# Attention in front of two MoE layers: 1/rms by a GpSimd power, and k^T v of two heads in the two halves of TensorE's columns

## The chip, the cores and the metric

One core of a Trainium2 chip runs the whole program. The time is in microseconds (us) of device time, from the start of the program to its end; lower is better. Before the change it is 1328.89 us (median of three runs, 1328.19 to 1331.12).

## What is computed

Three layers follow one another. The attention has no softmax; for 8 batches and 8 heads of 576 rows and 64 columns it is

```python
kv  = np.einsum('bhsd,bhse->bhde', k, v)          # 64 x 64 for each head
out = np.einsum('bhsd,bhde->bhse', q, kv)
rms = np.sqrt(np.mean(out * out, axis=-1, keepdims=True) + 1e-06)
x   = out / rms * g_norm                          # over the 64 columns of a head
```

Its result, 4608 tokens of 512 columns, goes through a first layer (h = x @ w_in, g = h * cos(h), g @ w_out, inner width 2048) and a second one (width 1024, with a softmax gate and a layer norm). Everything is float32.

## The kernel before

The program is one long list of tasks. Each task names its engine, an estimated duration, the buffers that it reads and writes, and a due time `at`. A planner (`Flow.run`) plays the list on model engines: of the tasks that can start first on an engine it takes the one with the earliest due time, and it emits the instructions in that order. On the chip every engine then runs its own list strictly in that order, and waits at an instruction whose data are not there yet. So an estimate in the planner sets an order and nothing else.

The two layers run over blocks of 512 tokens: 36 steps for each quarter of the first layer's inner width, four such passes, then 18 pairs of token tiles for the second layer. The attention is cut into slots, which the planner spreads over the first pass (`run_slots`, SLOTS per step), so that the attention of later tokens runs beside the first layer of earlier ones. Two kinds of slot matter here.

`kv_slots` (line 346) makes k^T v of a batch. The 8 heads are 4 pairs; the 64 columns of a pair's two heads stand side by side in 128 columns. One product of 128x128 therefore gives both heads' 64x64 blocks on its diagonal and two blocks that nobody needs. The 576 rows of a pair are five products (L358 four times, L360 once). All four pairs of a batch share one PSUM bank, and two ScalarE copies (L368) take the diagonal blocks out into `kvf`, whose other blocks are zero.

`tile_slots` (line 393) makes two tiles of 128 tokens. Each tile has a bank: q times kvf (L416), a square on ScalarE (L421), a sum over each head on VectorE (L422). Then, for both tiles at once, 1/rms on VectorE: two instructions that make a first guess (L429, L430) and three Newton rounds of three (L434, L437, L440), eleven in all on 128x16 elements. Then for each tile VectorE scales the products into `xn` (L458), TensorE transposes them back into the same bank (L463), and ScalarE takes the result out with the factor g (L469). The bank is free after that.

Banks are given out in turn by `next_bank` (line 341): the first six come from the four accumulators and the two banks named o and s, all later ones alternate between o and s. In the trace o and s are called ps_o, the accumulators ps_acc, the first layer's h ps_h; most buffers of the attention are called att, the spare ones xt.

For each block, `prep_x` splits x into a high and a low part (L564 on ScalarE, L569 on VectorE for the first three blocks and on GpSimd after that). `weights` turns the stored weights into float32 (L502 to L514) and splits them (L525, L527). A power on GpSimd is already used in the second layer, on 128x1 elements (L756).

Of the kernel before, what the change touches and what calls it, by code (L numbers as in the profile page):

```python
# [10 lines left out]
I32 = mybir.dt.int32  # L11
# [29 lines left out]
INV_2PI = float(1.0 / (2.0 * math.pi))  # L41
MAGIC = float(0x5F3759DF)

TINY = 0.17

# [17 lines left out]
class Flow:  # L63
# [92 lines left out]
def tile_kernel(ctx, tc, qkv, tail, g2, w1, w2, gl, out):  # L156
# [31 lines left out]
    for key in ("g2", "halfpi"):  # L188
        declare("const", key, 0, [P, 1])
    declare("const", "mhalf", 0, [P, 1])  # L190
    declare("const", "gl", 0, [P, NC])
# [27 lines left out]
    declare("att", "xn", 2, [P, DM])  # L219
    for n in ("ss", "y", "yt"):  # L220
        declare("att", n, 2, [P, 2 * H])

# [118 lines left out]
    def next_bank():  # L341
        n_bank[0] += 1
        early = ACC + ["o", "s"]
        return early[n_bank[0] - 1] if n_bank[0] <= len(early) else ("o", "s")[n_bank[0] % 2]

    def kv_slots(b):

        bk, n = next_bank(), ("kvf", b % 2)
        pairs = [("kvp", b, p) for p in range(NPAIR)]

        def slot(p):
# [10 lines left out]
            def copy(e):  # L362
                r = slice(e * D, (e + 1) * D)

                def blocks(key_):
                    return buf[key_][r, :].rearrange("p (n w) -> p n w", w=P)[:, :, r]

                ACT.copy(out=blocks(n), in_=blocks(bk))  # L368

            def run(at):  # L370
                kv_load(j, at - (ATT_LEAD if b else 0))
                if b == 0:
                    q_load(j, at)
                add("PE", 1.12, mm, r=[kv, tl] + ([bk] if p else []), w=[pairs[p]] + ([] if p else [bk]), at=at)
                if p == NPAIR - 1:
                    for e in range(2):
                        add("ACT", 0.4, lambda e=e: copy(e), r=[bk, *pairs], w=[("kvfh", n, e)] + ([n] if e == 0 else []), at=at)

            return run

        return [slot(p) for p in range(NPAIR)]

# [10 lines left out]
    def tile_slots(g):  # L393


        i = g % 2
        bks = [next_bank() for _ in range(2)]
        ss, y, yt = ("ss", i), ("y", i), ("yt", i)
        halves = [("ssh", g, h) for h in range(2)]

# [3 lines left out]
        def first(h, at):  # L404
            t, bk, sq = 2 * g + h, bks[h], stage()
            for b, a, n, row in parts(t):
# [6 lines left out]
                def mm(b=b, a=a, n=n, row=row, qs=qs, kvf=kvf):  # L413
                    for p in range(NPAIR):
# [3 lines left out]

                add("PE", 0.89, mm, r=[kvf, ("kvfh", kvf, 0), ("kvfh", kvf, 1), *qs], w=[bk], at=at)
            at -= PRI  # L420
            add("ACT", 0.61, lambda: ACT.activation(out=buf[sq], in_=buf[bk], func=AF.Square), r=[bk], w=[sq], at=at)  # L421
            add("DVE", 0.66, lambda: DVE.tensor_reduce(out=buf[ss][:, h * H:(h + 1) * H], in_=heads(buf[sq]), axis=AX.X,  # L422
                                                       op=ALU.add), r=[sq] + ([ss] if h else []),
                w=[halves[h]] + ([] if h else [ss]), at=at)


        def newton(at):
            def start():
                DVE.tensor_scalar(out=buf[ss], in0=buf[ss], scalar1=1.0 / D, scalar2=1e-6, op0=ALU.mult, op1=ALU.add)  # L429
                DVE.tensor_scalar(out=buf[y].bitcast(I32), in0=buf[ss].bitcast(I32), scalar1=-0.5, scalar2=MAGIC,  # L430
                                  op0=ALU.mult, op1=ALU.add)

            def square():
                DVE.tensor_tensor(out=buf[yt], in0=buf[y], in1=buf[y], op=ALU.mult)  # L434

            def times():
                DVE.scalar_tensor_tensor(out=buf[yt], in0=buf[yt], scalar=-0.5, in1=buf[ss], op0=ALU.mult, op1=ALU.mult)  # L437

            def update():
                DVE.scalar_tensor_tensor(out=buf[y], in0=buf[yt], scalar=1.5, in1=buf[y], op0=ALU.add, op1=ALU.mult)  # L440

            def all_():
                start()
                for _ in range(3):
                    square()
                    times()
                    update()

            add("DVE", 11 * TINY, all_, r=[*halves, ss], w=[ss, y, yt], at=at)

        def second_(h, at):
            t, bk, xn = 2 * g + h, bks[h], ("xn", h)

# [3 lines left out]
            def norm():  # L457
                DVE.tensor_tensor(out=heads(buf[xn]), in0=heads(buf[bk]),  # L458
                                  in1=buf[y][:, h * H:(h + 1) * H].unsqueeze(2).to_broadcast([P, H, D]), op=ALU.mult)

# [5 lines left out]
            xk = [x for k in range(KC) for x in xkeys(k, t * P, P)]  # L466
            add("DVE", 0.71, norm, r=[bk, y], w=[xn], at=at, ps=True)
# [4 lines left out]
        def run0(at):  # L472
            first(0, at)

        def run1(at):
            first(1, at)
            newton(at - PRI)
            for h in range(2):
                second_(h, at - PRI)

        return [run0, run1]

# [401 lines left out]
    for i in range(NPASS * NSTEP):  # L884
# [115 lines left out]
```

## Time and profile before

| | us |
|---|---|
| median of three runs | 1328.89 |
| the profiled execution | 1329.38 |
| its span, first to last instruction | 1327.6 |
| TensorE busy | 1295.1 (98%) |
| VectorE busy | 927.8 (70%) |
| ScalarE busy | 676.7 (51%) |
| GpSimd busy | 385.6 (29%) |

A busy time is the time in which at least one instruction of the engine was under way; matmuls overlap in their pipeline, so the durations of single ones add up to more than that. A float32 product with float32 operands is two instructions in the trace (two pieces, each with its own weight load, PEld), so the 160 products of k^T v are 320 instructions. The granted clock (PEclk) is a share of 2.4 GHz: 1.00 is that, 0.50 is 1.2 GHz. The bracket at the end of a row is idle time of the engine just before it, and what ended it.

### The profile page before, as it was taken

What the parts mean: (1) busy time and instruction counts of PE and PEld (TensorE: products, weight loads), DVE (VectorE), ACT (ScalarE), POOL (GpSimd) and SP (SyncE); (2) the same over time, 40 slices, a digit from 0 to 9 for tenths busy, and PEclk for the clock granted to TensorE, in tenths of its full rate; (3) what the DMA queues carried; (4) which work ended last, traced back from release to release, by engine and by line L of the source; (5) the groups of instructions that cost most, each with busy time, mean ns of one, the idle gap of its engine ahead of it and who ended that gap; (6) DMA issues with size and microseconds to landing.
All of it is one profiled execution on the core that took longest, in us unless ns stands there. A gap on an engine that the chain in (4) does not pass through costs nothing.

```text
span 1327.6 us, 17232 instructions
## 1 busy us (share of the span) xinstructions
PE 1295.1 (98%) x6148; PEld 1077.8 (81%) x6148; DVE 927.8 (70%) x1620; ACT 676.7 (51%) x1195; POOL 385.6 (29%) x364
## 2 busy tenths in 40 slices
PE   6789899999999999999999999999999999999998
PEld 6678788888888888888888888888788888888886
DVE  5889556588986456754545677878987878787853
ACT  3556445467655445545444555555554544444432
POOL 0001212036663225523131456443232212121100
PEclk9899999999999999999999999999999999999999
DMA  8643244323544243423232535464110111010000
GB/s 299 206 140 115 84 147 131 101 96 96 171 146 135 72 119 113 149 68 123 79 112 87 151 109 159 142 213 137 67 46 35 56 56 46 35 56 25 16 32 32
DMA packets 61830, 139.54 MB, mean 105 GB/s; under 512 B 7344, under 2 KB 9392, under 8 KB 60592
## 3 DMA queue, kind: packets, MB, share of 16 engines
q1 hardware_dynamic: 61744, 138.44, 32.4%
q8 instruction: 48, 0.79, 0.2%
q14 instruction: 38, 0.31, 0.1%
HBM read 91.23 MB, written 47.19 MB: 104 GB/s over the span
## 4 chain that ended last, share of the span: by engine, by line
PE 86%; DVE 6%; DMA 3%; ACT 2%; issue 1%; SPq 0%; POOL 0%; ACTq 0%; DVEq 0%
PE ps_acc L176 13%; PE ps_acc L174 13%; PE ps_acc L175 13%; PE ps_h L174 13%; PE ps_h L176 12%; PE ps_h L175 12%; PE ps_acc L773 2%; PE ps_o L416 2%; PE ps_o L358 2%; DMA xt<-w 2%; PE ps_o L463 1%; DVE att L440 1%; DVE att L437 1%; DVE att L434 1%; DMA xt<-qkv 1%
## 5 line engine op out<-in xcount | busy, mean ns | idle before, releaser
L569 POOL TENSOR_TENSOR xhl<-xt,xhl 128x512 fp32r<-128x512 f32 (+3 forms) x176 | 191.6, 1118 | 360.1 <-ACT xhl L564 359.9
L174 PE MATMUL ps_acc<-temps,wpool 128*128 128x512 f32 x648 | 254.5, 393 | 0.0
L176 PE MATMUL ps_acc<-temps,wpool 128*128 128x512 f32 x648 | 252.5, 390 | 0.0
L175 PE MATMUL ps_acc<-temps,wpool 128*128 128x512 f32 x648 | 252.5, 390 | 0.0
L174 PE MATMUL ps_h<-xhl,wpool 128*128 128x512 f32 x576 | 227.0, 394 | 0.5 <-ACT xhl L564 0.3
L175 PE MATMUL ps_h<-xhl,wpool 128*128 128x512 f32 x576 | 224.6, 390 | 0.2 <-DVE xhl L569 0.2
L176 PE MATMUL ps_h<-xhl,wpool 128*128 128x512 f32 x576 | 224.5, 390 | 0.0
L594 DVE SCALAR_TENSOR_TENSOR temps<-ps_h,temps 128x512 f32<-128x512 f32 x144 | 99.1, 688 | 112.3 <-ACT temps L592 111.8
L603 DVE TENSOR_TENSOR temps<-temps,temps 128x512 fp32r<-128x512 f32 x144 | 122.1, 848 | 69.7 <-ACT temps L602 69.0
L597 ACT ACTIVATE temps<-temps,const 128x512 f32<-128x512 f32 x144 | 104.2, 724 | 94.4 <-DVE temps L594 94.2
L592 ACT ACTIVATE temps<-ps_h 128x512 int32<-128x512 f32 x144 | 85.8, 596 | 129.0 <-PE ps_h L176 128.1
L600 DVE TENSOR_TENSOR temps<-ps_h,temps 128x512 f32<-128x512 f32 x144 | 99.0, 687 | 65.5 <-ACT temps L597 65.3
L176 PEld LDWEIGHTS ps_acc<-temps,wpool 128*128 128x128 f32 x648 | 121.8, 188 | 25.5
L174 PEld LDWEIGHTS ps_acc<-temps,wpool 128*128 128x128 f32 x648 | 122.0, 188 | 24.9 <-DVE temps L630 0.3
L175 PEld LDWEIGHTS ps_acc<-temps,wpool 128*128 128x128 f32 x648 | 121.9, 188 | 24.6
L602 ACT CAST temps<-temps 128x512 fp32r<-128x512 f32 x144 | 89.4, 621 | 100.2 <-DVE temps L600 90.9
L174 PEld LDWEIGHTS ps_h<-xhl,wpool 128*128 128x128 f32 x576 | 108.3, 188 | 23.4 <-issue 0.7
L176 PEld LDWEIGHTS ps_h<-xhl,wpool 128*128 128x128 f32 x576 | 108.2, 188 | 22.6
L175 PEld LDWEIGHTS ps_h<-xhl,wpool 128*128 128x128 f32 x576 | 108.4, 188 | 22.2 <-DVE xhl L569 0.5
L564 ACT CAST xhl<-xt 128x512 fp32r<-128x512 f32 (+3 forms) x192 | 90.8, 512 | 12.8 <-PE ps_h L176 11.9
L756 POOL TENSOR_TENSOR xt<-xt,const 128x1 f32<-128x1 f32 x36 | 23.0, 638 | 196.8 <-DVE xt L753 189.3
L779 DVE TENSOR_TENSOR wpool<-ps_acc,wpool 128x512 fp32r<-128x512 f32 x72 | 46.6, 686 | 42.6 <-ACT wpool L776 42.6
(140 smaller groups left out, 2259.2 us busy)
## 6 DMA issues: line engine op xcount, KB each, us to landing
px<-temps SPq DMA_DIRECT2D x144, 256.0 KB, 2.6
temps<-px SPq DMA_DIRECT2D x108, 256.0 KB, 3.9
xt<-w SPq DMA_DIRECT2D x28, 512.0 KB, 3.9
att<-qkv SPq DMA_DIRECT2D x24, 512.0 KB, 4.7
rawp<-w SPq DMA_DIRECT2D x20, 512.0 KB, 3.8
xt<-px SPq DMA_DIRECT2D x9, 1024.0 KB, 5.1
out<-temps SPq DMA_DIRECT2D x36, 256.0 KB, 2.0
att<-qkv SPq DMA_DIRECT2D x28, 288.0 KB, 5.3
```

Of the source, the lines that this page charges most:

```text
L174: PE.matmul(ps, lhsT=lh, rhs=rh, start=start, stop=False)
L175: PE.matmul(ps, lhsT=lh, rhs=rl, start=False, stop=False)
L176: PE.matmul(ps, lhsT=ll, rhs=rh, start=False, stop=stop)
L564: ACT.copy(out=buf["xh", i][:, k, a - m * TB:a - m * TB + n], in_=xt(k, a, n))
L569: eng.tensor_tensor(out=buf["xl", i][:, k, r], in0=xt(k, a, n), in1=f(buf["xh", i][:, k, r]), op=ALU.subtract)
L592: add("ACT", 0.61, lambda: ACT.activation(out=buf["kk"], in_=h(), func=AF.Copy, scale=INV_2PI, bias=0.25), r=[hb], w=["kk"], at=at)
L594: add("DVE", 0.71, lambda: DVE.scalar_tensor_tensor(out=buf[tk], in0=h(), scalar=INV_2PI, in1=buf["kk"], op0=ALU.mult, op1=ALU.subtract), ...
L597: add("ACT", 0.74, lambda: ACT.activation(out=buf[tk], in_=buf[tk], func=AF.Sin, bias=buf["halfpi"][:, 0:1], scale=2 * math.pi), r=[tk, "h ...
L600: add("DVE", 0.71, lambda: DVE.tensor_tensor(out=buf[tk], in0=h(), in1=buf[tk], op=ALU.mult), r=[hb, tk], w=[tk], at=at, ps=True)
L602: add("ACT", 0.64, lambda: ACT.copy(out=buf[ghk], in_=buf[tk]), r=[tk], w=[ghk], at=at + 2)
L603: add("DVE", 0.71, lambda: DVE.tensor_tensor(out=buf[glk], in0=buf[tk], in1=f(buf[ghk]), op=ALU.subtract), r=[tk, ghk], w=[glk], at=at + 2)
L779: DVE.tensor_tensor(out=buf["ll", n][:, part, :], in0=tr(), in1=f(buf["lh", n][:, part, :]), op=ALU.subtract)
```

## The change

k^T v is now made head by head. Each product takes the 64 columns of one head's k as weights and 64 columns of v as the moving operand; head 0 of a pair writes to PSUM partitions 0 to 63 (the first half of TensorE's columns), head 1 to 64 to 127, and the two heads alternate. A pair is ten products of 64x64 in place of five of 128x128, and nothing unneeded is made. Two pairs share a bank, so a batch has two slots and two banks in place of four slots and one bank, and two ScalarE copies for each bank. The planner's estimate for a pair goes from 1.12 to 0.62 us.

1/rms is made for each tile by itself, on GpSimd: an add of 1e-6 and a power with exponent -0.5, each on 128x8 elements, 2.0 us for both in the planner's book. The factor 1/64 has gone into the square's scale. The eleven VectorE instructions are gone. A slot is now one tile, not two, and SLOTS goes from 2 to 1.5 for each step.

```diff
-SLOTS0, SLOT_T, SLOT_D, SLOTS, CV_FIRST = 8, -12, 1, 2, 10
+POW = 2.0
+SLOTS0, SLOT_T, SLOT_D, SLOTS, CV_FIRST = 8, -12, 1, 1.5, 10
+KV_T = 0.62
...
-        t.port = eng == "POOL" or (eng == "DVE" and not ps)
+        t.port = eng in ("POOL", "DVE") and not ps
...
     def kv_slots(b):
-        bk, n = next_bank(), ("kvf", b % 2)
+        n, bks = ("kvf", b % 2), [next_bank() for _ in range(2)]
...
             def mm():
-                st, tl_, ps = buf[kv], buf[tl], buf[bk][:, p * P:(p + 1) * P]
-                for c in range(4):
-                    PE.matmul(ps, lhsT=st[:, c * P:(c + 1) * P],
-                              rhs=st[:, 512 + c * P:512 + (c + 1) * P], start=(c == 0), stop=False)
-                PE.matmul(ps, lhsT=tl_[:, 0:P], rhs=tl_[:, P:256], start=False, stop=True)
+                for c in range(5):
+                    for e in range(2):
+                        k_, v_ = (buf[tl], P) if c == 4 else (buf[kv], 512)
+                        at_ = e * D if c == 4 else c * P + e * D
+                        PE.matmul(buf[bk][e * D:(e + 1) * D, p % 2 * D:(p % 2 + 1) * D], lhsT=k_[:, at_:at_ + D],
+                                  rhs=k_[:, v_ + at_:v_ + at_ + D], start=(c == 0), stop=(c == 4))
...
+        def slot(half):
             def run(at):
+                bk = bks[half]
+                done = [("kvp", b, p) for p in range(2 * half, 2 * half + 2)]
+                for i, d in enumerate(done):
+                    pair(bk, 2 * half + i, [d], at)
+                for e in range(2):
+                    r = slice(e * D, (e + 1) * D)
+
+                    def copy(r=r):
+                        ACT.copy(out=buf[n][r, half * 256:half * 256 + 256].rearrange("p (n w) -> p n w", w=P)[:, :, r],
+                                 in_=buf[bk][r, 0:P].rearrange("p (n w) -> p n w", w=D))
...
+        return [slot(half) for half in range(2)]
...
-            add("DVE", 11 * TINY, all_, r=[*halves, ss], w=[ss, y, yt], at=at)
+            add("ACT", 0.61, lambda: ACT.activation(out=buf[sq], in_=buf[bk], func=AF.Square, scale=D ** -0.5),
+                r=[bk], w=[sq], at=at)
...
+        def rms(h, at):
+            i = (2 * g + h) % 4
+
+            def power():
+                POOL.tensor_scalar(out=buf["ss", i], in0=buf["ss", i], scalar1=1e-6, scalar2=None, op0=ALU.add)
+                POOL.tensor_tensor(out=buf["y", i], in0=buf["ss", i], in1=buf["mhalf"], op=ALU.pow)
+
+            add("POOL", POW, power, r=["mhalf"], w=[("ss", i), ("y", i)], at=at, ps=True)
...
-            run_slots(SLOTS, at, d / SLOTS)
+            run_slots(int(SLOTS * (i + 1)) - int(SLOTS * i), at, d / SLOTS)
```

What this does to the engines' lists shows at three places.

TensorE, from the first transposes of the attention on. In the names, const_65 is the identity, att_116 and att_117 are `xn`, att_104 to att_107 and xt_0_82 are the loaded k and v, ps_o and ps_acc the banks. Before:

```order
L463 MATMUL ps_acc_128<-const_65,att_116 128x128 x4
L358 MATMUL ps_o_135<-att_104 128x128 x4
L360 MATMUL ps_o_135<-att_106 128x128
L463 MATMUL ps_acc_129<-const_65,att_117 128x128 x4
L358 MATMUL ps_o_135<-att_105 128x128 x4
L360 MATMUL ps_o_135<-att_107 128x128
L463 MATMUL ps_acc_130<-const_65,att_116 128x128 x4
```

And now:

```order
L449 MATMUL ps_acc_131<-const_65,att_116 128x128 x4
L449 MATMUL ps_acc_132<-const_65,att_117 128x128 x4
L449 MATMUL ps_o_136<-const_65,att_116 128x128 x4
L449 MATMUL ps_o_137<-const_65,att_117 128x128 x4
L360 MATMUL ps_o_137<-att_104 64x64 x8
L360 MATMUL ps_o_137<-att_106 64x64 x2
L360 MATMUL ps_o_137<-att_105 64x64 x8
L360 MATMUL ps_o_137<-att_107 64x64 x2
L360 MATMUL ps_o_136<-xt_0_82 64x64 x10
L174 MATMUL ps_h_141<-xhl_90,wpool_69 128x512
```

The second batch's k^T v stood between the transposes of the first four tiles; now it stands behind all four, in the two banks that the third and the fourth tile leave. Over the whole list the 320 short products stand in 18 runs of 10 to 40 that follow one another without a product of full width between them. With the tiles that straddle two batches (64x128, six runs before) there are 25 runs in half columns.

VectorE, from the first sum over heads on. Here att_118 to att_121 are the sums, att_120 to att_123 before and att_122 to att_125 now the results y, xt_0_86 the weights under conversion. Before:

```order
L422 TENSOR_REDUCE att_119<-temps_99 128x8
L429 TENSOR_SCALAR att_118<-att_118 128x16
L430 TENSOR_SCALAR att_120<-att_118 128x16
L434 TENSOR_TENSOR att_122<-att_120 128x16
L437 SCALAR_TENSOR_TENSOR att_122<-att_122,att_118 128x16
L440 SCALAR_TENSOR_TENSOR att_120<-att_122,att_120 128x16
...
L422 TENSOR_REDUCE att_119<-temps_100 128x8
L458 TENSOR_TENSOR att_116<-ps_acc_128,att_120 128x512
L458 TENSOR_TENSOR att_117<-ps_acc_129,att_120 128x512
```

And now:

```order
L425 TENSOR_REDUCE att_118<-temps_97 128x8
L489 TENSOR_SCALAR xt_0_86<-xt_0_86 128x512
L491 SCALAR_TENSOR_TENSOR xt_0_86<-xt_0_86 128x512
L425 TENSOR_REDUCE att_119<-temps_98 128x8
L425 TENSOR_REDUCE att_120<-temps_99 128x8
L444 TENSOR_TENSOR att_116<-ps_acc_131,att_122 128x512
L425 TENSOR_REDUCE att_121<-temps_100 128x8
L494 TENSOR_SCALAR xt_0_86<-xt_0_86 128x512
L444 TENSOR_TENSOR att_117<-ps_acc_132,att_123 128x512
```

A tile's scaling now stands by itself, with sums and weight conversions between one and the next.

GpSimd, in whose list nothing stood between the identity and the first weight split (L527, later than 100 us); now the first 17 tiles' powers stand there, and from the eighteenth on they stand between the splits:

```order
L432 TENSOR_SCALAR att_118<-att_118 128x8
L433 TENSOR_TENSOR att_122<-att_118,const_63 128x8
L512 TENSOR_TENSOR wpool_70<-xt_0_86,wpool_70 128x512 x2
L554 TENSOR_TENSOR xhl_91<-xt_0_78,xhl_91 128x512
L432 TENSOR_SCALAR att_119<-att_119 128x8
L433 TENSOR_TENSOR att_123<-att_119,const_63 128x8
L554 TENSOR_TENSOR xhl_91<-xt_0_78,xhl_91 128x512 x3
```

So 36 adds and 36 powers are new on GpSimd, and some have up to three splits of 128x512 ahead of them.

## Rows read from the trace of the kernel before

**Rows 1.** Busy time of each engine by stretch, with instructions, TensorE's clock, DMA

```profile
core 0: us, PE busy (x) PEld busy (x) DVE busy (x) ACT busy (x) POOL busy (x), PEclk, DMA share, GB/s
0.00:25.00 25.00, 14.27 (x80) 13.09 (x81) 10.07 (x34) 6.09 (x10) 0.70 (x6) 0.97 0.94 318
25.00:150.00 125.00, 109.84 (x610) 93.37 (x610) 103.06 (x228) 69.86 (x125) 10.13 (x8) 0.92 0.46 151
150.00:300.00 150.00, 149.14 (x829) 126.39 (x828) 91.43 (x200) 81.74 (x153) 29.28 (x30) 1.00 0.35 115
300.00:1327.60 1027.60, 1021.81 (x4634) 844.97 (x4633) 723.29 (x1159) 519.05 (x910) 345.47 (x321) 1.00 0.29 93
```

**Rows 2.** Waits of TensorE, 0 to 160 us: waiter, releaser, total us, times, longest

```profile
PE ps_o L463 <- DVE att L458: 9.2, 3, 5.2
PE ps_acc L463 <- DVE att L458: 4.0, 1, 4.0
PE ps_o L463 <- ACT wpool L525: 2.7, 1, 2.7
PE ps_o L463 <- ACT temps L602: 2.3, 1, 2.3
```

**Rows 3.** Timeline of TensorE from 28.5 us: start, us, line, tiles, count

```profile
28.57 1.06 PE L358 MATMUL ps_o<-xt 128*128 128x128 f32 x8
...
29.68 0.60 PE L463 MATMUL ps_o<-const,att 128*128 128x128 f32 x4
```

**Rows 4.** Timeline of TensorE and its weight loads at a tile of two batches

```profile
34.48 1.14 PE L416 MATMUL ps_o<-att,att 128*64 128x128 f32 x12
35.46 0.60 PE L416 MATMUL ps_o<-att,xt 128*64 128x128 f32 x4
...
34.86 0.52 PEld L416 LDWEIGHTS ps_o<-att,att 128*64 128x64 f32 x8
```

**Rows 5.** Timeline of TensorE into and out of eight pieces in one half

```profile
176.55 0.39 PE L360 MATMUL ps_o<-att 128*128 128x128 f32 x2
176.87 1.09 PE L416 MATMUL ps_o<-att,att 128*64 128x128 f32 x8
177.89 0.50 PE L174 MATMUL ps_h<-xhl,wpool 128*128 128x512 f32 x1
```

**Rows 6.** Timeline of TensorE: the wait at the transposes after 135 us

```profile
134.89 0.39 PE L176 MATMUL ps_h<-xhl,wpool 128*128 128x512 f32 x1
138.89 1.71 PE L463 MATMUL ps_o<-const,att 128*128 128x128 f32 x8 [3.61 <-DVE att L458]
```

**Rows 7.** Groups of instructions on GpSimd: busy us, mean ns, idle before

```profile
L569 POOL TENSOR_TENSOR xhl<-xt,xhl 128x512 fp32r<-128x512 f32 x88 | 119.9, 1388 | 237.2 <-ACT xhl L564 237.1
L569 POOL TENSOR_TENSOR xhl<-xt,xhl 128x128 fp32r<-128x128 f32 x28 | 17.2, 613 | 16.4 <-ACT xhl L564 16.4
L756 POOL TENSOR_TENSOR xt<-xt,const 128x1 f32<-128x1 f32 x36 | 23.0, 638 | 196.8 <-DVE xt L753 189.3 <-DVE xt L743 7.4
```

**Rows 8.** Timeline of VectorE at the longest wait, first sum to scaling

```profile
47.02 0.69 DVE L422 TENSOR_REDUCE att<-temps 128x8 f32<-128x512 f32 x1 [1.56 <-ACT temps L421]
...
48.38 0.69 DVE L422 TENSOR_REDUCE att<-temps 128x8 f32<-128x512 f32 x1
...
49.32 0.17 DVE L429 TENSOR_SCALAR att<-att 128x16 f32<-128x16 f32 x1
...
51.41 0.17 DVE L440 SCALAR_TENSOR_TENSOR att<-att,att 128x16 f32<-128x16 f32 x1
...
52.10 1.28 DVE L458 TENSOR_TENSOR att<-ps_o,att 128x512 f32<-128x512 f32 x2
```

**Rows 9.** Timelines of VectorE and of GpSimd, 132 to 138 us

```profile
132.58 1.20 DVE L440 SCALAR_TENSOR_TENSOR att<-att,att 128x16 f32<-128x16 f32 x1
...
132.45 2.56 POOL L569 TENSOR_TENSOR xhl<-xt,xhl 128x512 fp32r<-128x512 f32 x2 [2.36 <-ACT xhl L564]
```

**Rows 10.** Group of the copies out of the k^T v bank

```profile
L368 ACT COPY att<-ps_o 64x256 f32<-64x256 f32 x14 | 5.1, 366 | 9.9 <-PE ps_o L360 9.7
```

More of the change, by code (lines that the diff above doesn't have):

```diff
@@ L189, in tile_kernel @@
         declare("const", key, 0, [P, 1])
-    declare("const", "mhalf", 0, [P, 1])
+    declare("const", "mhalf", 0, [P, H])
     declare("const", "gl", 0, [P, NC])
@@ L219, in tile_kernel @@
     declare("att", "xn", 2, [P, DM])
-    for n in ("ss", "y", "yt"):
-        declare("att", n, 2, [P, 2 * H])
+    for n in ("ss", "y"):
+        declare("att", n, 4, [P, H])
     for pool, i, n_st, n_y, n_f in (("spare1", "a", 2, 2, 2), ("rawp", "b", 2, 2, 2), ("late_x0", "c", 1, 1, 6)):
@@ L346, in kv_slots, with pair @@
     def kv_slots(b):
-        bk, n = next_bank(), ("kvf", b % 2)
-        pairs = [("kvp", b, p) for p in range(NPAIR)]
-        def slot(p):
+        n, bks = ("kvf", b % 2), [next_bank() for _ in range(2)]
+        def pair(bk, p, w, at):
             j = b * NPAIR + p
@@ L370, in run @@
-            def run(at):
[L371 to L377, printed above, removed]
+                for c in range(5):
[4 more added lines that the diff above has]
+                                  rhs=k_[:, v_ + at_:v_ + at_ + D], start=(c == 0), stop=(c == 4))
@@ new lines, in pair @@
+            kv_load(j, at - (ATT_LEAD if b else 0))
+            if b == 0:
+                q_load(j, at)
+            add("PE", KV_T, mm, r=[kv, tl] + ([bk] if p % 2 else []), w=w + ([] if p % 2 else [bk]), at=at)
+        def slot(half):
+            def run(at):
+                bk = bks[half]
[7 more added lines that the diff above has]
+                                 in_=buf[bk][r, 0:P].rearrange("p (n w) -> p n w", w=D))
+                    add("ACT", 0.35, copy, r=[bk, *done] + ([n] if half or e else []),
+                        w=[("kvfh", n, half, e)] + ([] if half or e else [n]), at=at)
@@ L379, in slot @@
             return run
-        return [slot(p) for p in range(NPAIR)]
+        return [slot(half) for half in range(2)]
     def parts(t):
@@ L393, in tile_slots @@
     def tile_slots(g):
-        i = g % 2
         bks = [next_bank() for _ in range(2)]
-        ss, y, yt = ("ss", i), ("y", i), ("yt", i)
-        halves = [("ssh", g, h) for h in range(2)]
         def heads(ap):
@@ L404, in first @@
         def first(h, at):
-            t, bk, sq = 2 * g + h, bks[h], stage()
+            t, i, bk, sq = 2 * g + h, (2 * g + h) % 4, bks[h], stage()
             for b, a, n, row in parts(t):
@@ L417, in mm @@
                                   start=True, stop=True)
-                add("PE", 0.89, mm, r=[kvf, ("kvfh", kvf, 0), ("kvfh", kvf, 1), *qs], w=[bk], at=at)
+                add("PE", 0.89, mm, r=[kvf, *(("kvfh", kvf, i, e) for i in range(2) for e in range(2)), *qs], w=[bk], at=at)
             at -= PRI
[L421 to L424, printed above, removed]
@@ L427, in newton @@
[L427 to L447, printed above, removed]
-            add("DVE", 11 * TINY, all_, r=[*halves, ss], w=[ss, y, yt], at=at)
+            add("ACT", 0.61, lambda: ACT.activation(out=buf[sq], in_=buf[bk], func=AF.Square, scale=D ** -0.5),
+                r=[bk], w=[sq], at=at)
@@ new lines, in first @@
+            add("DVE", 0.66, lambda: DVE.tensor_reduce(out=buf["ss", i], in_=heads(buf[sq]), axis=AX.X, op=ALU.add),
+                r=[sq], w=[("ss", i)], at=at)
+        def rms(h, at):
[4 more added lines that the diff above has]
+            add("POOL", POW, power, r=["mhalf"], w=[("ss", i), ("y", i)], at=at, ps=True)
@@ L451, in second_ @@
         def second_(h, at):
-            t, bk, xn = 2 * g + h, bks[h], ("xn", h)
+            t, i, bk, xn = 2 * g + h, (2 * g + h) % 4, bks[h], ("xn", h)
             def tr():
@@ L458, in norm @@
                 DVE.tensor_tensor(out=heads(buf[xn]), in0=heads(buf[bk]),
-                                  in1=buf[y][:, h * H:(h + 1) * H].unsqueeze(2).to_broadcast([P, H, D]), op=ALU.mult)
+                                  in1=buf["y", i].unsqueeze(2).to_broadcast([P, H, D]), op=ALU.mult)
             def turn():
@@ L466, in second_ @@
             xk = [x for k in range(KC) for x in xkeys(k, t * P, P)]
-            add("DVE", 0.71, norm, r=[bk, y], w=[xn], at=at, ps=True)
+            add("DVE", 0.71, norm, r=[bk, ("y", i)], w=[xn], at=at, ps=True)
             add("PE", 0.42, turn, r=[xn, "ident"], w=[bk], at=at)
@@ L470, in second_, with slot, run @@
                                                     scale=buf["g2"][:, 0:1]), r=[bk, "g2"], w=xk, at=at)
[L472 to L478, printed above, removed]
+        def slot(h):
+            def run(at):
+                first(h, at)
+                rms(h, at - PRI)
                 second_(h, at - PRI)
-        return [run0, run1]
+            return run
+        return [slot(h) for h in range(2)]
     def pair_engine(on_dve):
```

7 lines of the change are left out of this document (removed).

## Prediction

> **What bounds the kernel now.** I read the busy times by stretch first, because the share over the whole span mixes two regimes [rows 1]. From 150 us on TensorE has no holes: 149.14 of 150 us busy, then 1021.81 of 1027.60. There a microsecond of TensorE's work is a microsecond of the result, and nothing that VectorE or GpSimd is spared counts. Before 150 us it is different. TensorE is idle for 25 - 14.27 = 10.7 us in the first stretch, where the first k and v are loaded (DMA share 0.94), and for 125 - 109.84 = 15.2 us in the second, where VectorE is busy for 103.06 of 125 us and the granted clock is 0.92 on average.
>
> The waits say what those idle times are [rows 2]. Six waits at the transposes L463 hold 9.2 + 4.0 + 2.7 + 2.3 = 18.2 us of the 25.9. The two put down to ScalarE stand before the same transposes, which need VectorE's scaling L458 too. The longest is 5.2 us, another is 3.6 us [rows 6], so the third of the first row is 0.4 us. The rest of the idle time is mostly the load at the start, which the change leaves alone. So there are two accounts: TensorE's work, and the early waits for sum, 1/rms and scaling.
>
> **TensorE's work: the products.** Ten pieces of a pair follow one another at 29.68 - 28.57 = 1.11 us, 0.111 us each [rows 3]. Before there are 320 pieces: 320 x 0.111 = 35.5 us (more where the clock is low; that scales both sides, and I leave it out).
>
> After there are 640 pieces, half as wide in weights and in moving columns. No row shows such a piece, so I take it from two things. A piece with half the weights but all 128 moving columns takes 0.11 us in its stream: eight of them last 1.09 us, less 0.27 for the last one's own length and 0.05 for the first weight load, over seven steps [rows 5]. So the stream goes by the moving columns, and 64 of them should take 0.055 us. The second thing is whether the two halves run side by side. The tile that straddles two batches has eight pieces in one half and then eight in the other: they last from 34.48 to 35.46 + 0.60 = 36.06, 1.58 us [rows 4]. One after the other they would take 1.09 + 8 x 0.11 = 1.97. The missing 0.39 us are three to four pieces that ran beside others. In that stretch eight weight loads of 0.14 us start within (0.52 - 0.14) = 0.38 us, one each 0.054 us, twice the rate of one half alone. With the heads alternating from the first piece I take full overlap: 640 x 0.055 / 2 = 17.6 us. The other end is no overlap: 640 x 0.055 = 35.2 us. I take the first because the overlap shown began as soon as the other half's pieces came up.
>
> Those rows only show the engine issuing a piece with its weights each 0.054 us, not each 0.027. The Trainium skill ("TensorE: Matmul & The Clock Gate", section "Wait — 56ns, not 53.3ns?") speaks against this change: with hardware decode off its sequencer spends about 62 ns on each MATMUL, and that binds once the array's work is shorter. By that rule 640 pieces take 39.7 us, an estimate, more than the 35.5 before; the rows, at 0.054 us for sixteen pieces that may have been queued, neither show it nor exclude it.
>
> **TensorE's work: into and out of half columns.** From the end of the last full piece (176.55 + 0.39 = 176.94) to the end of the first full piece after the run (177.89 + 0.50 = 178.39) are 1.45 us [rows 5]. Eight steps of 0.11 and one of 0.22 (1021.81 us for 4634 instructions, nearly all full-width [rows 1]) are 1.10. So one visit to half columns costs 0.35 us. The order has 25 runs in half columns where six stood: 19 x 0.35 = 6.6 us, on the path. The account of the products is 17.6 + 6.6 - 35.5 = **-11.3 us**.
>
> **1/rms.** VectorE loses eleven instructions for each of 18 pairs of tiles, from 49.32 to 51.58 at the wait shown [rows 8], 2.3 us when nothing disturbs them. After 150 us that is worth nothing, since TensorE covers it. Before, what counts is the way from a pair's first sum to the end of its second scaling: 52.10 + 1.28 - 47.02 = 6.4 us [rows 8].
>
> The new way goes over GpSimd, which does add and power for each tile. Its price is not in the trace. An elementwise instruction there costs (1388 - 613) / 384 = 2.0 ns for each element and 355 ns besides [rows 7]. The power on one element takes 638 ns, so 283 ns over the fixed part. If that is paid for each element, eight cost 355 + 8 x 283 = 2.6 us, with the add (0.37) 3.0 us. If it is paid once, 1.0 us for both. I take the middle, 2.0 us, since neither row is nearer. Two tiles in turn then need 0.7 + 2 x 2.0 + 0.7 = 5.4 us, 1.0 less than now.
>
> That shortens four of the six waits by 1.0 us each and takes the 0.4 us one. The wait of 3.6 us goes whole: there four of the small VectorE instructions took 1.2 us, not 0.17, beside a GpSimd split of x [rows 9], and none of them is left. Against it stands the start: the second batch's k^T v stood between the first transposes and now comes behind them, in the banks of the third and fourth tile; four pairs of 0.55 us that filled waits no longer do, +2.0 us. Together -4.0 - 0.4 - 3.6 + 2.0 = **-6.0 us**. If a power with its add costs 1.0 us, the way is 3.4 us, the four waits lose up to 3.0 each (11.0 together), and this is -13; at 3.0 us it is 7.4 us, and the sum turns to +4.0 - 0.4 - 3.6 + 2.0 = about +2.
>
> **The clock.** At 0.92 in the second stretch some 0.08 x 110 = 9 us are lost to it [rows 1], in and after the idle times. A third of the waits gone brings a part of that back: **-1.0 us** (0 to -3).
>
> **Edits at nothing.** Twice as many copies out of the k^T v banks, each half as large: 0.37 us now [rows 10], so at most 16 x 0.37 = 5.9 us more on ScalarE, which is busy for 69.86 of 125 us and has room; without that cover at most 0.4 us at the first batch's last copy. SP issues as many transfers as before, with two loads of q moved ahead of the second weight load: at most one 288 KB load, 0.9 us at 318 GB/s. The square's scale, the smaller sums and `mhalf` cost nothing new. GpSimd gets 36 x 2.0 = 72 us more in the first 300 us, where it has 29.28 of 150 busy in the second half.
>
> **Sum.** -11.3 - 6.0 - 1.0 = -18.3 us against the profiled execution's 1329.38 us (its span is 1327.6, with 1.8 around it; the median of the runs is 0.5 lower): **1311 us**. With the bounds of the power it runs from -11.3 - 13 - 2 (1303) to -11.3 + 2 (1320).
>
> **The rivals.**
>
> *Every early wait goes: 1297 us.* If VectorE's backlog rather than the way through 1/rms sets the six waits, sparing it lets all 18.2 us go and 3 us of clock: 1329.4 - 11.3 - 18.2 - 3. For it: VectorE's 103 of 125 us. Against it: each tile still waits for its own square, sum, power and scaling, with only two banks.
>
> *A floor for each piece: 1329 us.* The change doesn't do what it says if a short piece still needs 0.055 us of the whole engine, from its weight load or its issue. Then 35.2 + 6.6 - 35.5 = +6.3 us eats the early gain of 7.0. For it: no row has pieces closer than 0.054 us. Against it: in those same rows the rate is just what two streams of 0.11 give. By the rule cited above this case would end at about 1333 us.
>
> *The power comes later than the order allows: slower, 1336 us.* TensorE runs its list in order, and the order puts a tile's transposes where 2.0 us on GpSimd make them ready. Each microsecond more stops TensorE there, with the first layer's products queued behind. At 3.0 us and 36 tiles that is up to 36 us; half of it, with the rest under other work, gives 1329.4 - 11.3 + 18. It decides from (11.3 + 2.7) / 36 = 0.4 us of lateness a tile if all is exposed. For it: the dear end of the price, and up to three splits of 1.39 us ahead of some powers [rows 7]. Against it: after 150 us the old order, whose VectorE instructions came late too, cost TensorE less than 1 us [rows 1].
>
> **How the numbers follow.** The forecast has 0.60, all waits gone 0.10, the floor 0.15, the late power 0.15. About 0.2% (2.7 us) is what a measurement of this kernel can tell from no change. Faster: 0.60 + 0.10 + 0.04 of the floor = 0.74. Same: 0.09 of the floor and 0.01 of the late power = 0.10. Slower: 0.02 + 0.14 = 0.16. The likeliest case's own range is 1303 to 1320. The range from 1299 to 1333 takes in the floor and leaves out half of the case below (0.05) and most of the late power (0.11).
>
> **What would show it.** Right: 640 pieces for k^T v, a pair's twenty in about 0.55 us, two weight loads of one moment; 0.35 us lost around a run; a power on 128x8 of 1 to 2.6 us; the six waits at the transposes down to about 12 us in all. The forecast is wrong if the pieces stand 0.055 us apart, if TensorE gets new idle times after 150 us that end with a scaling, or if the time before 150 us grows.

## The result, and the profile after

The changed kernel takes **1307.45 us** (median of four runs, 1305.68 to 1308.45) beside 1329.04 us for the kernel before: 0.984 of it, with an interval of 0.9826 to 0.9851. The prediction was 1311 us with a range from 1299 to 1333.

The profiled execution took 1306.71 us, its span 1304.6. First the busy times of the whole span:

```profile
PE 1278.2 (98%) x6468; PEld 1058.4 (81%) x6468; DVE 881.9 (68%) x1421; ACT 681.3 (52%) x1211; POOL 461.6 (35%) x437
```

TensorE's share is 98% before and after, and says nothing. Busy and idle time apart say more. Busy time fell from 1295.1 to 1278.2 us (-16.9), idle time from 1327.6 - 1295.1 = 32.5 to 1304.6 - 1278.2 = 26.4 us (-6.1). Together they are the 23.0 us of the spans (21.6 in the medians). The view by stretch, with the columns of [rows 1], says where:

```profile
0.00:25.00 25.00, 12.71 (x120) 11.43 (x120) 8.59 (x20) 7.20 (x13) 7.28 (x13) 1.00 0.95 319
25.00:150.00 125.00, 116.72 (x931) 96.75 (x933) 89.23 (x152) 80.06 (x154) 54.14 (x52) 0.96 0.51 167
150.00:300.00 150.00, 149.93 (x893) 124.20 (x890) 83.58 (x118) 90.54 (x164) 70.37 (x63) 1.00 0.38 120
300.00:1304.60 1004.60, 998.87 (x4534) 826.04 (x4532) 700.53 (x1133) 503.54 (x882) 329.79 (x310) 1.00 0.29 92
```

Against [rows 1], TensorE's idle time goes from 10.7 to 12.3 us in the first stretch, from 15.2 to 8.3 in the second, from 0.86 to 0.07 in the third, and stays nearly the same in the last (5.8 and 5.7). The clock of the second stretch goes from 0.92 to 0.96. VectorE has 14 us less to do there and GpSimd 44 more, and GpSimd's load went from 29.28 to 70.37 us between 150 and 300 us without a hole in TensorE.

**The products.** TensorE's timeline (start, us, line, tiles, count) at a run of two pairs, and at two runs of one pair:

```profile
112.77 0.40 PE L176 MATMUL ps_acc<-temps,wpool 128*128 128x512 f32 x1
113.10 1.39 PE L360 MATMUL ps_o<-att 128*64 128x64 f32 x40
114.41 0.50 PE L174 MATMUL ps_h<-xhl,wpool 128*128 128x512 f32 x1
...
51.40 0.80 PE L360 MATMUL ps_o<-att 128*64 128x64 f32 x20 [0.83 <-ACT xt L455]
...
52.72 0.80 PE L360 MATMUL ps_o<-att 128*64 128x64 f32 x20
```

Forty pieces last 1.39 us and twenty 0.80, so twenty take 0.59 us, **0.0295 us a piece**; what is left of 0.80 is the last piece's own length. From the end of the last full piece (112.77 + 0.40 = 113.17) to the end of the first full one behind the run (114.41 + 0.50 = 114.91) are 1.74 us; less 1.18 for the pieces and 0.22 for one full step this is **0.34 us for the visit**. The 32 pairs and the 19 more visits cost 32 x 0.59 + 19 x 0.34 = 25.3 us in place of 35.5.

**The waits.** TensorE's waits from 0 to 160 us (waiter, releaser, total us, times, longest):

```profile
PE ps_acc L360 <- DMA att<-qkv: 6.9, 2, 4.9
PE ps_o L449 <- DVE att L444: 5.3, 3, 2.4
PE ps_o L418 <- ACT xt L455: 2.3, 3, 1.2
PE ps_acc L449 <- DVE att L444: 2.3, 2, 1.2
PE ps_acc L360 <- DMA xt<-qkv: 2.2, 2, 1.1
PE ps_o L360 <- ACT xt L455: 1.6, 2, 0.8
```

The transposes are L449 now. The 18.2 us of [rows 2] are 5.3 + 2.3 = 7.6. Behind them stand 2.3 + 1.6 = 3.9 us of a new kind: the next user of a bank waits for ScalarE to take the transposed tile out. The first and the fifth row are the load at the start, 6.9 + 2.2 = 9.1 us; in the same view of the kernel before it is

```profile
PE ps_acc L358 <- DMA att<-qkv: 5.7, 2, 4.9
```

The first batch's products end sooner now, and TensorE waits for the next pair's k and v instead.

**GpSimd.** The power and its add (duration min/median/max in ns, first and last start):

```profile
L433 POOL TENSOR_TENSOR att<-att,const x36: 1667/1668/2135, 18.3 to 250.4; 128x8 f32<-128x8 f32 x36
L432 POOL TENSOR_SCALAR att<-att x36: 240/245/616, 17.9 to 249.7; 128x8 f32<-128x8 f32 x36
```

With 0.08 us between them a tile takes 2.0 us, what the planner's book says.

**The start** is where the change costs: the waits for the load are 3.4 us longer, and the first four transposes wait one by one. TensorE's timeline shows them:

```profile
21.76 0.63 PE L449 MATMUL ps_acc<-const,att 128*128 128x128 f32 x4 [1.20 <-DVE att L444]
23.45 0.63 PE L449 MATMUL ps_acc<-const,att 128*128 128x128 f32 x4 [1.06 <-DVE att L444]
25.53 0.63 PE L449 MATMUL ps_o<-const,att 128*128 128x128 f32 x4 [1.45 <-DVE att L444]
27.61 1.09 PE L449 MATMUL ps_o<-const,att 128*128 128x128 f32 x4 [1.45 <-DVE att L444]
29.47 2.40 PE L360 MATMUL ps_o<-att 128*64 128x64 f32 x40 [0.78 <-ACT xt L455]
...
25.00:30.00 5.00, 2.25 (x18) 1.67 (x20) 4.59 (x8) 2.44 (x5) 1.67 (x1) 0.62 0.42 137
```

(The last row is the view by stretch.) They come at 1.7 to 2.1 us, the pace of four powers in turn, and each wait ends with the scaling behind one of them. With the wait behind them they hold 1.20 + 1.06 + 1.45 + 1.45 + 0.78 = 5.9 us, where one wait of 4.0 us stood [rows 2]. After these holes the granted clock of 25 to 30 us is 0.62.

**The clock.** These are the stretches with a granted clock of 0.50 (1.2 GHz), five in the kernel before and two now, and one row of TensorE's timeline before the first of them, of the kernel before and of the changed one:

```profile
23.32:26.73 3.41, 3.33 (x16) 3.36 (x17) 3.07 (x14) 0.69 (x1) 0.00 (x0) 0.50 0.67 211
43.80:47.22 3.42, 3.39 (x17) 3.00 (x16) 1.86 (x5) 1.94 (x4) 0.00 (x0) 0.50 0.56 167
50.63:57.45 6.82, 4.51 (x20) 4.22 (x21) 6.37 (x15) 3.36 (x6) 0.00 (x0) 0.50 0.28 80
84.76:88.17 3.41, 3.41 (x14) 3.12 (x15) 3.41 (x9) 3.41 (x10) 0.00 (x0) 0.50 0.17 30
139.37:142.79 3.42, 3.42 (x15) 3.02 (x14) 1.35 (x3) 2.08 (x4) 0.00 (x0) 0.50 0.00 0
...
26.15:32.98 6.83, 4.61 (x66) 4.11 (x65) 6.19 (x11) 4.97 (x10) 0.58 (x1) 0.50 0.30 103
63.70:67.11 3.41, 3.28 (x14) 3.18 (x15) 2.16 (x4) 1.67 (x4) 0.00 (x0) 0.50 0.73 251
...
10.83 2.08 PE L358 MATMUL ps_acc<-xt 128*128 128x128 f32 x8
...
14.37 3.78 PE L418 MATMUL ps_acc<-att,att 128*128 128x128 f32 x16
```

Each of the seven comes behind one or more waits of TensorE. It was busy in them for 18.1 us before and for 7.9 now. Its first pieces run at half the pace too, although the column has 1.00 there: eight take 2.08 us that take 1.06 in [rows 3]. That lasts until about 13 us before (7.3 us of TensorE's work) and about 19 us now (10.2 us). Of 25.3 and 18.1 us at the lower level half is lost, 12.7 and 9.1 us, an estimate from these rows: the clock gives back 3.6 us.

### The profile page after: what moved, and what is told of

Same layout as the page of the kernel before. It is cut to its first block, busy times and chain, and to the rows that moved or that the text cites. A ratio compares the mean times of both kernels' runs of the same rounds, so it can differ in the third digit from the quotient of the medians.

```text
span 1304.6 us, 17778 instructions
## 1 busy us (share of the span) xinstructions
PE 1278.2 (98%) x6468; PEld 1058.4 (81%) x6468; DVE 881.9 (68%) x1421; ACT 681.3 (52%) x1211; POOL 461.6 (35%) x437
## 4 chain that ended last, share of the span: by engine, by line
PE 92%; DMA 2%; DVE 2%; ACT 1%; POOL 1%; issue 1%; SPq 0%; ACTq 0%; DVEq 0%
PE ps_acc L174 14%; PE ps_acc L176 14%; PE ps_acc L175 14%; PE ps_h L174 14%; PE ps_h L176 14%; PE ps_h L175 14%; PE ps_o L418 2%; PE ps_acc L758 2%; PE ps_o L360 2%; DMA xt<-w 1%; PE ps_o L449 1%; POOL att L433 1%; DMA xt<-qkv 1%; DMA px<-temps 1%; DVE temps L615 0%
```

## The experiments

Eleven kernels ran, with the kernel before beside them each time: 1328.3 to 1329.2 us.

### Each half of the change alone

The first is the kernel before with new products only, the second the changed kernel with the old products.

```diff
...
-                for c in range(4):
-                    PE.matmul(ps, lhsT=st[:, c * P:(c + 1) * P], ...
+                for c in range(5):
+                    for e in range(2):
...
+                        PE.matmul(buf[bk][e * D:(e + 1) * D, p * P + e * D:p * P + (e + 1) * D],
+                                  lhsT=k_[:, at_:at_ + D], rhs=k_[:, v_ + at_:v_ + at_ + D],
...
```

> The kernel before with only the products changed: ten 64x64 products of a pair, heads alternating between the halves, in the old bank and slots; 1/rms stays on VectorE. Theory (the account of TensorE's work is real and adds to the early waits): 640 pieces at 0.029 us, as the changed kernel's rows have them, are 18.6 us for 35.5; 21 visits to half columns where six stood cost 15 x 0.35 = 5.3 us; so -11.6 us, 1317 us. Rival (before 150 us the waits fill up whatever TensorE saves): only the four tenths of the products that stand after 150 us count, -4.7 us, 1324 us.

> The changed kernel with the old 128x128 products, and all else as it is, the order of the instructions too: two pairs to a bank, tiles by themselves, the power on GpSimd. Theory: 16.9 us of products come back and 18 visits to half columns at 0.35 us go, +10.6 us on the changed kernel's 1307.5, so 1318 us, and the six early waits stay as short as in the changed kernel (about 11 us of idle time at the transposes and products). Rival (the gain is nearly all VectorE's): within 3 us of the changed kernel, 1310 us.

Halves alone: 1316.98 us, 0.9909 [0.9894, 0.9924], -12.1. The rest alone: 1315.38 us, 0.9895 [0.9879, 0.9912], -13.7. The second stretch by view, halves alone first:

```profile
25.00:150.00 125.00, 107.32 (x825) 89.60 (x826) 105.40 (x246) 72.54 (x132) 10.52 (x8) 0.95 0.49 161
...
25.00:150.00 125.00, 117.69 (x706) 101.81 (x707) 88.12 (x150) 78.47 (x151) 53.97 (x52) 0.96 0.50 162
```

With halves alone TensorE works less there and is idle for 17.7 us, more than the 15.2 before: the longest wait at its transposes is 6.5 us where it was 5.2, and one of 3.0 us for a copy out of the k^T v bank is new. Without halves it is idle for 7.3. So the products are worth 12.1 us by themselves and 21.6 - 13.7 = 7.9 beside the rest (1/rms on GpSimd, tiles by themselves, two banks: these three were not run apart), the rest 13.7 by itself and 21.6 - 12.1 = 9.5 beside the products. The prediction's -11.3 lies within the first pair; its -6.0 - 1.0 for 1/rms and clock is smaller than both of the second. The two halves add up to 25.8 us, 4.2 more than the change gave. The clock is enough for that: TensorE works at the lower level for 18.6 us with halves alone and for 14.3 without them, so by the estimate above the two save 3.4 and 5.5 us of it, and both together only 3.6.

### Do the two halves run side by side?

Two kernels keep the pieces and change only where and in which order they run. One puts both heads into the first half of the columns; the other keeps the two halves, but makes the first head's ten pieces and then the second's.

```diff
-                for c in range(5):
-                    for e in range(2):
+                for e in range(2):
+                    for c in range(5):
...
-                        PE.matmul(buf[bk][e * D:(e + 1) * D, ...
+                        PE.matmul(buf[bk][0:D, ...
```

(The last pair of lines is in the first kernel only.)

> The changed kernel with the same 640 pieces, but both heads of a pair in the first half of the columns, one head's ten after the other's; the copies fetch the second head from there. Same order of instructions. Theory (a piece of 64 columns takes 0.055 us of its half, and the gain to 0.029 is the two halves side by side): a pair takes 1.1 us, 16.6 us more in all, 1324 us. Rival (each piece has a floor of 0.029 us of the whole engine, whichever half it is in): a pair stays at 0.58 us and the time at 1308 us.

> The changed kernel with the same 640 pieces in the same halves and the same place in the order, but a pair's first head with its ten pieces first, and the second head's ten after them. Theory (the halves run side by side, but only as far ahead as TensorE looks, some three to four pieces as in the old straddling tile): each change from one head to the next saves about 3.5 x 0.055 us, a pair takes 0.8 us in place of 0.58, +7 us, 1315 us. Rival (a floor of 0.029 us a piece, not the two halves): 1308 us as before this edit.

One half: 1323.08 us, 0.9955 [0.994, 0.997], 15.6 us over the changed kernel. Heads in turn: 1316.83 us, 0.9906 [0.9893, 0.992], 9.4 us over it. The timelines of the two, one half first, have a run of one pair and one of two:

```profile
55.89 1.38 PE L360 MATMUL ps_o<-att 128*64 128x64 f32 x20
58.09 2.54 PE L360 MATMUL ps_o<-xt 128*64 128x64 f32 x40
...
56.13 1.20 PE L360 MATMUL ps_o<-att 128*64 128x64 f32 x20
58.16 2.01 PE L360 MATMUL ps_o<-xt 128*64 128x64 f32 x40
```

In one half twenty more pieces take 2.54 - 1.38 = 1.16 us, 0.058 each, twice the 0.0295 of the changed kernel. So the halves do run side by side, at full overlap, when their pieces alternate. With heads in turn a pair alone takes 1.20 against 0.80: the second half's pieces start only when the last few of the first half are left. Nine runs of two pairs at 2.01 - 1.39 = 0.62 and seven of one at 0.40 make 8.4 us; the seven pairs at the start, in two longer runs, bring it near the 9.4. So 9.4 us hang on the order of two loops.

### Does VectorE's work matter, or the way through GpSimd?

The changed kernel with eleven Newton instructions for each tile on VectorE (booked at 1.87 us) in place of the add and the power:

```diff
-                POOL.tensor_scalar(out=buf["ss", i], ...
-                POOL.tensor_tensor(out=buf["y", i], in0=buf["ss", i], in1=buf["mhalf"], op=ALU.pow)
+                DVE.tensor_scalar(out=ss, ...
+                DVE.tensor_scalar(out=y.bitcast(I32), ...
+                for _ in range(3):
+                    DVE.tensor_tensor(out=yt, in0=y, in1=y, op=ALU.mult)
+                    DVE.scalar_tensor_tensor(out=yt, in0=yt, scalar=-0.5, in1=ss, ...
+                    DVE.scalar_tensor_tensor(out=y, in0=yt, scalar=1.5, in1=y, ...
```

> The changed kernel with 1/rms made by the old eleven VectorE instructions, for each tile by itself on 128x8 elements; products in halves as in the change. VectorE gets 36 x 11 small instructions at about 0.2 us, twice as many as before the change. Theory (the early gain is VectorE's room): TensorE's idle time between 25 and 150 us is at least the old 15 us, the clock there falls to 0.92 again, 1307.5 + 7 + 4 = 1318 us or more. Rival (the early gain comes from taking tiles by themselves, in smaller slots): idle time as in the changed kernel, 8 us, and 1308 to 1310 us.

1342.37 us, 1.0105 [1.0087, 1.0122]: slower than the kernel before, and 35 us over the changed one. The direction is the theory's, the size is not. The view by stretch, and the timelines of VectorE and of GpSimd:

```profile
25.00:150.00 125.00, 103.71 (x776) 85.24 (x775) 107.89 (x314) 69.25 (x129) 7.27 (x6) 0.89 0.47 154
150.00:300.00 150.00, 142.05 (x898) 115.65 (x897) 110.10 (x297) 78.71 (x149) 30.69 (x32) 0.97 0.30 98
...
159.98 0.50 DVE L434 TENSOR_SCALAR att<-att 128x8 f32<-128x8 f32 x1
...
161.90 0.67 DVE L439 SCALAR_TENSOR_TENSOR att<-att,att 128x8 f32<-128x8 f32 x1
162.59 0.17 DVE L440 SCALAR_TENSOR_TENSOR att<-att,att 128x8 f32<-128x8 f32 x1
...
165.83 0.17 DVE L440 SCALAR_TENSOR_TENSOR att<-att,att 128x8 f32<-128x8 f32 x1
...
159.71 2.83 POOL L561 TENSOR_TENSOR xhl<-xt,xhl 128x256 fp32r<-128x256 f32 x4 [8.65 <-ACT xhl L556]
162.75 2.83 POOL L561 TENSOR_TENSOR xhl<-xt,xhl 128x256 fp32r<-128x256 f32 x4 [0.21 <-ACT xhl L556]
```

An instruction of 0.17 us takes 0.66 while GpSimd splits x, and the next one, between two groups of splits, 0.17 again; the eleven of this tile last from 159.98 to 166.00, 6.0 us in place of the 2.2 without a neighbour. Two more tiles lose as much, three lose about 1 us, and thirty take the 2.2 us. TensorE loses 8 us after 150 us, where it lost less than one with the old pairs and with the power. Earlier, from 25 to 150 us, it is idle for 21.3 us in place of 8.3 at a clock of 0.89 in place of 0.96, with VectorE busy for 107.89 us. So tiles by themselves are no gain with this 1/rms, which is 0.3 us over its booked time undisturbed and 4 us beside such splits. Whether the early loss comes from these 0.3 us or from VectorE's load, no run separates.

### What does a late power cost?

The power twice, first with the book left at 2.0 us for a tile, then with 3.7:

```diff
                 POOL.tensor_tensor(out=buf["y", i], in0=buf["ss", i], in1=buf["mhalf"], op=ALU.pow)
+                POOL.tensor_tensor(out=buf["y", i], in0=buf["ss", i], in1=buf["mhalf"], op=ALU.pow)
...
-POW = 2.0
+POW = 3.7
```

> The changed kernel with each tile's power done twice on GpSimd (the same result written again), the planner's book and the order unchanged: 36 x 1.7 = 61 us more on GpSimd, each tile 1.7 us later than the order reckons with. Theory (GpSimd's power is on the way only before 150 us, where TensorE waits for the first dozen or so tiles; later it is covered): about 10 tiles x 1.7 us, 1320 to 1326 us, and no new idle time of TensorE after 150 us. Rival (a power that is late stops TensorE at every tile, with half of it exposed): +31 us, 1338 us. Second rival (GpSimd is free of charge): 1308 us.

> The changed kernel with the power done twice, as in the run that took 1356.3 us, but with the planner's book saying 3.7 us for a tile's add and powers where it says 2.0, so that the order of every engine is made for the longer way. Theory (the 49 us of that run came from an order that puts a tile's transposes where the shorter power would have made them ready): the order now puts first-layer work between, TensorE stays busy between 150 and 300 us (over 147 of 150), only the waits before 150 us grow, and the time is 1312 to 1324 us. Rival (the two banks that the tiles take in turn can't be given back faster whatever the order): 1345 us or more, with TensorE busy for less than 140 of 150 us there. Clear of both, 1325 to 1344: order and banks share it.

Not booked: 1356.32 us, 1.0203 [1.0188, 1.0217], 48.9 over the changed kernel; the theory fell, and the rival had the mechanism right and the price too small (31 us). Booked: 1317.16 us, 0.9914 [0.99, 0.9927]; here the theory held. The stretch from 150 us, TensorE's longest row of waits and a piece of its timeline in the first:

```profile
150.00:300.00 150.00, 129.94 (x848) 103.78 (x848) 55.87 (x83) 71.14 (x136) 84.81 (x77) 0.99 0.29 95
...
PE ps_o L450 <- DVE att L445: 39.6, 29, 4.1
...
202.66 0.63 PE L450 MATMUL ps_o<-const,att 128*128 128x128 f32 x4 [1.76 <-DVE att L445]
```

and the stretch and the same row of waits in the second:

```profile
150.00:300.00 150.00, 150.00 (x948) 123.75 (x947) 81.55 (x114) 90.39 (x168) 99.63 (x85) 1.00 0.37 116
...
PE ps_o L450 <- DVE att L445: 6.8, 3, 3.5
```

The instructions on GpSimd are the same in both, and so are the banks. Only the order differs: with the right book there is first-layer work between a tile's sum and its transposes, and the 29 waits are 3. What stays, 1317.16 - 1307.45 = 9.7 us, lies mostly before 150 us (from 25 us on busy for 111.90 of 125 us at a clock of 0.90, where the changed kernel has 116.72 and 0.96). The second power takes 1.64 us; a tile that is later than its book by that, 36 times, is 59 us of lateness. Of it 48.9 us, four fifths, came through, the lower clock counted in.

### Fewer visits

The four tiles that straddle two batches as one task each, with the pieces of the two halves in turn; then also a half's two pairs as one task:

```diff
-                add("PE", 0.89, mm, r=[kvf, ...], w=[bk], at=at)
+                todo.append((a, n, row, qs, kvf))
+            add("PE", 0.89, mm, r=reads, w=[bk], at=at)
...
-            add("PE", KV_T, mm, r=[kv, tl] + ([bk] if p % 2 else []), ...
+                add("PE", 2 * KV_T, lambda: [f_() for f_, _ in both], ...
```

> The changed kernel with the same idea used on the four tiles that straddle two batches: their two parts (64 rows each, one in each half of the columns) are one task now, and their pieces alternate. In the changed kernel three of these tiles make two visits of eight pieces (0.87 us each), the fourth sixteen pieces in 1.42 us. Theory: 3 x 0.87 + 0.5 us of pieces and one visit (25 to 24 by the order) go, -3.4 us, 1304 us. Rival (a tile now holds its bank until both batches' k^T v are there, or the new order costs as much): no gain, 1308 us or more.

> As the run before, and the two pairs that share a bank are one task of TensorE: 18 visits to half columns in place of 24. Theory (a visit costs 0.35 us on the path): 6 x 0.35 = 2.1 us below the run before, 1302 us. Rival (the pair that is loaded first now waits for the second, which costs as much as the visits): the same as the run before, or slower.

1304.91 us, 0.9818 [0.9804, 0.9831], and 1304.11 us, 0.9812 [0.9799, 0.9826]. In the two later straddling tiles of both, the next batch's q is loaded over q of the last batch that is still to be read, since six buffers don't hold eight pairs; that changes a part of the output, and the two times price the pieces only. The first edit was worth 2.5 us where 3.4 were expected; the second one's 0.8 is within the spread of the runs. Two more kernels take the second edit alone, and with it the first for the two early tiles, where nine buffers hold both batches' q:

> The changed kernel with the products of a half's two pairs as one task of TensorE, so that no other work comes between them: 21 runs in half columns where it has 25. Theory (0.35 us for each visit): 4 x 0.35 = 1.4 us less than the changed kernel's 1307.45, 1306.0. Rival (a visit's cost hides somewhere, or the longer task holds up the tiles): 1307.5 or more.

> The run before it with one edit more: in the two early tiles that straddle batches, where nine buffers of q hold both batches' four pairs, both parts are one task of TensorE with pieces of the one half and the other in turn; the two later straddling tiles stay as they are (six buffers of q don't hold eight pairs). Each such tile's sixteen pieces should take 8 x 0.11 = 0.9 us where they take 1.58, and one visit less is made: 2 x 0.4 + 0.35 = 1.2 us less, 1304.8 us. Rival: 1306 or more, if what is saved early is taken by waits there.

**1303.0 us** (1302.59 to 1303.78), 0.9809 [0.9795, 0.9822], the fastest kernel of the study; and 1306.33 us (1304.23 to 1307.49), 0.9829 [0.9816, 0.9842]. The first gave 4.4 us where four visits explain 1.4. The second lost 3.3 us on it where it should have won 1.2. The second stretch of the two:

```profile
25.00:150.00 125.00, 117.39 (x920) 97.40 (x920) 89.75 (x151) 82.79 (x159) 55.42 (x54) 0.96 0.51 168
...
25.00:150.00 125.00, 115.64 (x902) 94.96 (x902) 89.29 (x151) 79.83 (x153) 56.07 (x52) 0.94 0.49 159
```

The second has less to do there, is idle for 9.4 us in place of 7.6, and got a clock of 0.94 in place of 0.96; over its span the mean clock is 0.993 in place of 0.996. The clock is enough for the difference: TensorE works at the lower level for 14.4 us in the first kernel and for 23.3 in the second, 4.5 us of loss by the estimate above, where their profiled executions differ by 4.3. The second kernel's own five runs say the same: 1304.23 us at a mean clock of 0.997, 1305.91 to 1307.49 at 0.992 and 0.993. So its edit is neither confirmed nor refuted. The first kernel's 14.4 us are 3.7 less than the changed kernel's 18.1, which gives 1.9 of its 4.4 us; with 1.4 for the visits 1.1 are left. And the kernel with six visits less works at the lower level for 23.2 us where the run before it has 18.6, a loss of 2.3 us that hides what the visits save. Whether an order's waits or chance decide on the clock, these runs don't settle.

## Why the prediction was right

**Pieces.** Predicted 17.6 us for 640 at full overlap; measured 32 x 0.59 = 18.9. The one-half kernel excludes the other end. The rival's rule (the Trainium skill, "TensorE: Matmul & The Clock Gate", section "Wait — 56ns, not 53.3ns?", about 62 ns for each MATMUL with hardware decode off) doesn't bind here: the pieces stand 29.5 ns apart.

**Visits.** Predicted 0.35 us each, measured 0.34, and the number in the order was right. The Trainium skill ("TensorEngine Tiling (Array Packing)", section "Key Properties") says that a change of tiling mode drains TensorE; the row agrees in that 0.34 us are lost around a run, but doesn't show that a drain is what they are. The price rests on rows alone: the runs with fewer visits moved by 0.8 us for six and 4.4 for four, with the clock in both. The account of the products came to 25.3 - 35.5 = -10.2 us for the -11.3 predicted.

**The price of the power.** The middle of 1.0 and 3.0 us was taken, since neither row was nearer; the rows say 2.0. That it came out was luck, and it decided the case: 2.0 us is also what the planner's book says, and the run with a late power shows what a miss costs.

**The waits.** Predicted -4.0 - 0.4 - 3.6 = -8.0 and +2.0 at the start. Idle time fell by 6.9 + 0.8 = 7.7 us after 25 us and rose by 1.6 before: -6.1 for -6.0. But the way to it was in part another, and that the sums agree is in part luck. The +2.0 came as 5.9 - 4.0 = +1.9 at the first transposes. The load, of which the prediction said that the change leaves it alone, cost 9.1 - 5.7 = 3.4 us more. The pair's way became 51.59 - 45.64 = 5.95 us, not 5.4, as the next rows (VectorE's timeline around the pair of [rows 8]) show:

```profile
45.64 0.69 DVE L425 TENSOR_REDUCE att<-temps 128x8 f32<-128x512 f32 x1
...
48.82 0.69 DVE L444 TENSOR_TENSOR att<-ps_o,att 128x512 f32<-128x512 f32 x1
...
50.90 0.69 DVE L444 TENSOR_TENSOR att<-ps_o,att 128x512 f32<-128x512 f32 x1 [0.18 <-POOL att L433]
```

What helps is that the first tile's scaling doesn't wait for the second one's sum: it is done at 49.51, after 3.9 us. The waits at the transposes fell further than said (to 7.6, not 12), and 3.9 us came back as waits for ScalarE to free a bank.

**The clock** is the term that was mis-sized: -1.0 us, 0 to -3. By the estimate above it gave **-3.6**: 5.1 in the stretches behind 20 us (half of 18.1 - 7.9), less 1.5 for the longer start at half pace (half of 10.2 - 7.3). That start is not in the prediction's 9 us, which were read from the clock's column in [rows 1]. The step "a third of the waits gone brings a part of that back" failed in its size, and the runs don't say what the clock follows: halves alone has 0.95 in the second stretch with a wait of 6.5 us left, the twice-done power with the right book 0.90 with none over 3.5 us there. Why it rose stays open. Products -10.2, idle times -6.1 and clock -3.6 make -19.9 of the spans' -23.0; the other 3.1 us weren't found in a row.

**Edits at nothing.** The copies were right: 0.26 us each now, and TensorE doesn't wait for them.

```profile
L378 ACT COPY att<-ps_o 64x128 f32<-64x128 f32 x28 | 7.3, 261 | 8.1 <-PE ps_o L360 7.6
```

GpSimd's 72 us more were hidden, but for the early waits above, and only because the order knew of them.

**The rivals.** *Every early wait goes* fell: 7.6 us at the transposes stay. *A floor for each piece* fell by the one-half kernel. *The power comes later than the order allows* did not happen and was rightly the one on the other side: its mechanism is real, and was under-priced. Half of the lateness was to reach the end; four fifths did. With that share and the 21.6 us measured, it would decide from 21.6 / (36 x 0.83) = 0.7 us of lateness a tile, an estimate. The argument against it, that the old order hid late VectorE work after 150 us, was wrong: an order has room for the lateness it was made for, no more.

## What to carry to other kernels

Two products that are half as wide fill TensorE's columns together in full only if the instruction list alternates between the halves piece by piece; count the visits to half columns (0.34 us here) against the gain, and put them next to each other. Where engines run lists that a planner wrote, a duration in its book that is 1.6 us too small at each of 36 tiles cost 49 us, and the same work rightly booked 10: measure an operation before moving it to another engine, and book what was measured. And where two kernels differ by 1 to 4 us, look first at how long TensorE worked at its lower clock in each: here that was as large as the edit under test.

## What the runs showed of the hardware that was not expected

A power on GpSimd gets dearer with its elements: 638 ns for 128x1 [rows 7], 1668 ns for 128x8, some 147 ns for each further element in a partition, less than the 283 that one row alone suggested. TensorE lets pieces for the other half of the columns run ahead only a short way: of ten queued behind ten, the first ran early enough to save only 1.38 - 1.20 = 0.18 us, three pieces. VectorE's smallest instructions lose much beside GpSimd: 0.17 us became 0.66 beside splits of 128x256, and 1.20 beside those of 128x512 [rows 9]. And the granted clock's column can have 1.00 where the pieces go at half pace, as in the first 13 to 19 us here.
